# Order of the first loads in an attention and two-layer feed-forward kernel: queries in two parts, w_in ahead of the second batch's keys and values

## The chip, the core and the metric

The program runs on one core of one Trainium2 chip. The metric is the device time of one execution in microseconds (us), taken as the median of three runs. The engines are TensorE (PE, with its weight loads as PEld), VectorE (DVE), ScalarE (ACT), GpSimd (POOL) and SyncE (SP). SP issues nearly all DMA transfers, ACT a few; an engine takes its instructions in order.

## What is computed

Everything is float32 at the outside, the weights arrive as float64. Three stages follow one another:

```
k_p, v_p = mean of k, v over pools of 8 rows            # 576 rows -> 72
scores   = q @ k_p^T / sqrt(64); attn = softmax(scores)
x        = (attn @ v_p) laid out as 4608 tokens x 512    # 8 batches, 8 heads
h        = x @ w_in (512 x 2048);  g = h * cos(h);  y = g @ w_out
out      = (silu(y @ w_gate) * (y @ w_val)) @ w_out2
```

## The kernel before

Tokens are worked in nine blocks of 512, a batch has 576 of them. The first feed-forward layer runs as a list of slots (block, 128 columns of the hidden layer); the attention of the later batches is threaded between slots. The second layer follows. This document is about what comes ahead of slot 0 and about the first slots.

**Batches.** The code counts them from 0. The change's "batch 2" is index 1, written (1, ...) below. For batch 0 the queries come in by `load_q` (line 143): four transfers, for r and e in 0 and 1, each of 32 partitions and of rows of 32 floats (128 bytes). `ACT_QUEUE` (line 69) says which (batch, r) ACT issues, the rest go to SP. The keys and values of batch 0 go to `kst` and `vst`; those of batch 1 are loaded whole by `load_kv1` (line 171): four key tiles into the slots `wa30` to `wa33`, three value tiles into `wa20` to `wa22`, slots that later hold converted parts of w_in. Keys and values are pooled by adds on DVE (`pool_sum`, line 187). For batches 2 and up POOL does that.

**Tiles of attention.** Batch 0 has five tiles of queries. `do_qt` (254) transposes one on DVE, `do_s` (259) makes the scores on PE, their extreme on DVE and the exponentials on ACT, then come norms on DVE, transposes on PE with copies on ACT (`do_pt`), and the products with the values (`do_av`, 340) for a group of tiles, copied by ACT to `ring`. Scores, transposes and value products share two PSUM buffers. `x_split` (486) splits 512 tokens of `ring` into a high part (ACT) and a low part (DVE), and only then can `pe_h` (501), the first product of the feed-forward layer, run.

**Conversion of weights.** w_in and w_out are turned from float64 bits into float32 by hand: a unit is 128 rows by 512 columns, loaded by `cv_load` (432), then `cv_exp` and others on DVE, `cv_bias` and a copy on ACT. `conv` (952) is a generator over all units: eight of w_in ((0,0) to (0,3) and (1,0) to (1,3)), then w_out and w_in in turn. `fill(n)` (995) takes n steps of it, `fill_to` (999) goes on until a unit of w_in is done, `load_i(n)` (921) issues n units of w_in (two transfers of 256 KB each), `load_o(n)` (929) units of w_out. Slot 0 needs units (0,0) to (0,3); slots 4 to 7 need (1,0) to (1,3). Units (2,c) and (3,c) take the slots of the second batch's raw values and keys, so their load waits until those have been summed.

**Order.** The Python text gives a priority; a scheduler at build time sets each engine's order by priority and by when it believes operands to be ready, and puts in the waits, among them a wait of each transfer's issue for the landing of an earlier one that used the same semaphore. On the chip that order is fixed. The text ahead of slot 0 is lines 1008 to 1026, and then the string `program` (line 1057), whose words are calls: `s`, `x`, `p`, `a` for scores, norms, transposes and value products of batch 0; `V0 v` for its value sums; `f` and `F` for `fill` and `fill_to`; `i` and `o` for `load_i` and `load_o`; `X` for `x_split`; `q` for `load_q(1)`; `K` and `U` for the key and value sums of batch 1; `k` for its key transposes; `b` for the first load of batch 2.

Of the kernel before, what the change touches and what calls it, by code (L numbers as in the profile page):

```python
# [8 lines left out]
F32 = mybir.dt.float32  # L9
# [16 lines left out]
def fused_kernel(  # L26
# [18 lines left out]
    nc = tc.nc  # L45
    B, H, S, D = q.shape
# [3 lines left out]
    P = 128  # L50
    POOL = 8
    SP = S // POOL
    NP = H // 2
# [12 lines left out]
    LEAD = 4  # L66
    ACTB = 2
    Y32 = NF1
    ACT_QUEUE = {(0, 0), (3, 1), (1, 1), (3, 0), (1, 0)}

    const = ctx.enter_context(tc.tile_pool(name="const", bufs=1))
    chain = ctx.enter_context(tc.tile_pool(name="chain", bufs=2))
# [4 lines left out]
    p1a = tc.alloc_tile_pool(name="p1a", bufs=1, reuse_waits="tile")  # L77
# [62 lines left out]
    qt_in = {}  # L140
    qview = q.rearrange("b (r p) (t i) d -> b r i p t d", r=2, i=32)

    def load_q(b):
        qi = qt_in[b] = p1a.tile([P, NP, S], F32, name=f"qi_{b}", tag="qi")
        for r in range(2):
            for e in range(2):
                a = 32 * (2 * r + e)
                (nc.scalar if (b, r) in ACT_QUEUE else nc.sync).dma_start(
                    qi[a : a + 32].rearrange("i p (t d) -> i (p t) d", d=32),
                    qview[b, r, :, :, :, 32 * e : 32 * e + 32].rearrange("i p t d -> i (p t) d"),  # L150
                )

    kvraw = {}
    kraw1 = []
# [16 lines left out]
    def load_kv1():  # L171

        for p in range(NP):
            t = wts.tile([P, 2, TB], F32, name=f"k1_{p}", tag=f"wa3{p}")
            nc.sync.dma_start(t[:SP], kview[1][:, :, p].rearrange("r s x -> s r x"))
            kraw1.append(t[:SP])
        for j in range(0, NP + 1, 2):
            t = wts.tile([P, 2, TB], F32, name=f"v1_{j}", tag=f"wa2{j // 2}")
            for r in range(2):
                rows = t[r * SM : (r + 1) * SM]  # L180
                if j < NP:
                    nc.sync.dma_start(rows, vview[1][r, :, j : j + 2])
                else:
                    nc.sync.dma_start(rows[:, 0], vleft[1])
            vraw1.append((j, t[:, : min(2, NP + 1 - j)]))

    def pool_sum(eng, dst, raw):
        h = POOL * D // 2
        while h > D:
            eng.tensor_add(raw[..., :h], raw[..., :h], raw[..., h : 2 * h])  # L190
            h //= 2
        eng.tensor_add(dst, raw[..., :D], raw[..., D : 2 * D])
# [16 lines left out]
    def prep_k(b):  # L209

        kp = kps.pop(b)
        ps = psum.tile([P, NP, SP], F32, name=f"kps_{b}", tag="att", bufs=2)
        for p in range(NP):
            nc.tensor.transpose(ps[:, p], kp[:, p].rearrange("s r d -> s (r d)"), ident[:SP, :SP])
        nc.scalar.mul(kT[0:64, :, 0:SP], ps[0:64], -EXP_SCALE)
        nc.scalar.mul(kT[64:128, :, SP:], ps[64:128], -EXP_SCALE)
# [175 lines left out]
    def run_item(b, x):  # L392
        if x[0] == "s":
            do_s(b, x[1])
            if x[1] + 1 < len(TILES):
                do_qt(b, x[1] + 1)
        elif x[0] == "exp":
            do_exp(b, x[1])
        elif x[0] == "norm":
            do_norm(b, x[1])  # L400
        elif x[0] == "pt":
            do_pt(b, x[1])
        elif x[0] == "av":
            do_av(b, x[1], x[2])
            do_av(b, x[1], x[2] + 1)
        elif b + 1 < B:
            if x[0] == "q":
                load_q(b + 1)
            elif x[0] == "k":
                prep_k(b + 1)  # L410
            elif x[0] == "v":
                prep_v(b + 1)
            else:
                do_qt(b + 1, 0)
# [17 lines left out]
    def cv_load(key, src, home=None):  # L432
        st = raw_tile(f"st_{key}") if home is None else wts.tile([P, 2, TB], F32, name=f"st_{key}", tag=home)
        st = st.rearrange("p a t -> p (a t)")
        src = src if isinstance(src, list) else [src]
        m = P // len(src)
        for i, x in enumerate(src):
            nc.sync.dma_start(st[i * m : (i + 1) * m].bitcast(U64), x)
        cv[key] = st.rearrange("p (t two) -> p t two", two=2)
# [481 lines left out]
    def load_i(m):  # L921
        for _ in range(m):
            u = next(to_load_i, None)
            if u is not None:
                _, j, c = order[u]
                src = [w_in[(r * NP + c) * D : (r * NP + c + 1) * D, j * TB : (j + 1) * TB] for r in range(2)]
                cv_load(keys[u], src, f"wa{j}{c}")
# [67 lines left out]
    def fill(m):  # L995
        for _ in range(m):
            conv_done[0] = next(conv_ops, len(order))
# [12 lines left out]
        nc.sync.dma_start(kst4[:, r], kview[0][r])  # L1010
    load_i(1)
    fill(2)
    load_q(0)
    load_i(1)
    for r in range(2):
        nc.sync.dma_start(vst[r * SM : (r + 1) * SM, :NP], vview[0][r])
        nc.sync.dma_start(vst[r * SM : (r + 1) * SM, NP], vleft[0])
# [3 lines left out]
    for r in range(2):  # L1021
        pool_sum(nc.vector, kps[0][:, :, r], kst4[:, r])
    prep_k(0)
    load_kv1()
    load_i(1)
    fill(8)
    do_qt(0, 0)
    kfree = kst.rearrange("s h x -> s (h x)")
# [22 lines left out]
    def sum_v1():  # L1051
# [3 lines left out]


    program = (
        "s0 s1 f4 x0 s2 p0 V0 v x1 p1 f3 s3 a0 x2 p2 f3 x3 i1 p3 a1 w F3 X s4 i1 q o2 "
        "K0 K1 K2 K3 U0 x4 k b i3 f6 "
    )  # L1060
    steps = {
        "s": s_,
# [9 lines left out]
        "i": load_i,  # L1072
        "o": load_o,
        "q": lambda: load_q(1),
        "k": lambda: prep_k(1),
        "b": lambda: load_kv(*raws[0]),
# [22 lines left out]
    for i, s in enumerate(slots):  # L1099
        n, f = s  # L1100
# [157 lines left out]
```

## Time and profile before

| what | value |
|---|---|
| median of 3 runs | 1804.75 us (1804.24 to 1807.91) |
| profiled execution, its own time | 1804.83 us |
| its span in the profile | 1803.1 us |
| PE busy | 1737.5 us, 96% |
| DVE busy | 1263.8 us, 70% |
| ACT busy | 1066.6 us, 59% |

The span is what the profiler saw of the program; the time is the run's own and is 1.7 us longer. An engine's busy share is over the whole span; which engine holds up the others in a stretch has to be read from that stretch.

### The profile page before, as it was taken

To read this page: it belongs to the slowest core of one execution; us is meant where nothing else is said; L and a number is where in the kernel's file an instruction comes from. 1 tells how busy PE (TensorE), PEld (TensorE's weight loads), DVE (VectorE), ACT (ScalarE), POOL (GpSimd) and SP (SyncE) were. 2 spreads that over 40 slices of the span, in tenths; PEclk is the share of its full clock that TensorE was granted. 3 is DMA by queue.
4 is the path that set the end of the run, shared out by engine and by line. 5 is a ranking of instruction groups with operands and counts; after the bars stand their busy time and mean duration, and the time that the engine had idled before them with its cause. 6 is when DMAs were issued, how large, how long until landed. Compare 5 with 4: busy or idle time off the path is not lost.

```text
span 1803.1 us, 23421 instructions
## 1 busy us (share of the span) xinstructions
PE 1737.5 (96%) x8044; PEld 1439.4 (80%) x8044; DVE 1263.8 (70%) x2152; ACT 1066.6 (59%) x1933; POOL 171.7 (10%) x254
## 2 busy tenths in 40 slices
PE   2879999999999999999999999999999999999998
PEld 2546587888878888878877888888888888999998
DVE  6898688877877677787875586863584367358446
ACT  3578587777777767778776565533443344344333
POOL 0150513304104022000000000000000000000000
PEclk9989999999999999999999999999999999999999
DMA  9934246446566455474885488576667556787773
GB/s 186 203 104 120 79 165 188 156 131 197 148 205 218 114 198 144 158 220 153 235 275 176 159 320 291 193 252 225 194 200 267 193 192 221 290 265 246 294 249 93
DMA packets 248157, 357.01 MB, mean 198 GB/s; under 512 B 149608, under 2 KB 155752, under 8 KB 248040
## 3 DMA queue, kind: packets, MB, share of 16 engines
q1 hardware_dynamic: 224840, 352.58, 61.7%
q10 hardware_dynamic: 23200, 2.95, 1.1%
q8 instruction: 64, 1.05, 0.2%
q14 instruction: 53, 0.43, 0.1%
HBM read 285.74 MB, written 69.73 MB: 197 GB/s over the span
## 4 chain that ended last, share of the span: by engine, by line
PE 68%; DVE 14%; DMA 9%; ACT 5%; issue 2%; SPq 1%; POOL 0%; ACTq 0%; DVEq 0%
PE X L762 13%; PE oX L892 8%; PE Y L762 7%; PE h L507 4%; PE h L509 4%; PE h L508 4%; PE acc L578 4%; PE oY L892 4%; PE acc L579 4%; PE acc L577 4%; PE Z L762 3%; DMA w2r<-w_dram 2%; PE oZ L892 2%; PE av L358 2%; PE acc L570 2%
## 5 line engine op out<-in xcount | busy, mean ns | idle before, releaser
L762 PE MATMUL X<-t_P,wc 128*128 128x512 f32 (+1 forms) x1080 | 232.6, 367 | 1.0 <-ACT u L811 1.0
L507 PE MATMUL h<-xhl,wa 128*128 128x512 f32 x576 | 231.5, 402 | 0.0
L508 PE MATMUL h<-xhl,wa 128*128 128x512 f32 x576 | 226.3, 393 | 1.3 <-DVE xhl L131 1.3
L509 PE MATMUL h<-xhl,wa 128*128 128x512 f32 x576 | 225.6, 392 | 0.0
L762 PEld LDWEIGHTS X<-t_P,wc 128*128 128x128 f32 x1080 | 196.5, 188 | 27.5 <-ACT u L811 2.4
L578 PE MATMUL acc<-gl,wo_ring 128*128 128x512 f32 x448 | 176.4, 394 | 1.7 <-DVE gl L558 1.5
L577 PE MATMUL acc<-gh,wo_ring 128*128 128x512 f32 x448 | 175.1, 401 | 3.1 <-ACT gh L555 2.9
L579 PE MATMUL acc<-gh,wo_ring 128*128 128x512 f32 x448 | 175.4, 391 | 0.0
L544 DVE SCALAR_TENSOR_TENSOR w<-w,hs 128x512 f32<-128x512 f32 x144 | 102.3, 710 | 49.7 <-ACT w L541 48.4
L516 ACT ACTIVATE hs<-h 128x512 f32<-128x512 f32 x144 | 85.7, 595 | 76.4 <-DVE w L544 47.8
L540 ACT ACTIVATE w<-w 128x512 f32<-128x512 f32 x144 | 91.0, 632 | 64.9 <-DVE w L519 63.8
L507 PEld LDWEIGHTS h<-xhl,wa 128*128 128x128 f32 x576 | 108.7, 189 | 25.7 <-issue 4.1
L508 PEld LDWEIGHTS h<-xhl,wa 128*128 128x128 f32 x576 | 108.7, 189 | 25.3 <-issue 2.4
L509 PEld LDWEIGHTS h<-xhl,wa 128*128 128x128 f32 x576 | 108.5, 188 | 23.8 <-issue 0.9
L519 DVE SCALAR_TENSOR_TENSOR w<-w,hs 128x512 f32<-128x512 f32 x144 | 105.3, 731 | 23.7 <-ACT w L518 23.5
L814 DVE TENSOR_TENSOR p<-p,X 128x512 f32<-128x512 f32 (+1 forms) x60 | 37.9, 632 | 117.0 <-PE X L762 109.5
L558 DVE TENSOR_TENSOR gl<-w,gh 128x512 fp32r<-128x512 f32 x128 | 90.9, 710 | 40.2 <-ACT gh L555 38.6
L130 ACT CAST xhl<-pst 128x1024 fp32r<-128x1024 f32 (+1 forms) x70 | 67.7, 967 | 71.3 <-PE oX L892 26.1
L518 ACT ACTIVATE w<-hs,few 128x512 f32<-128x512 f32 x144 | 104.5, 725 | 7.3 <-DMA w_dram<-ce_w 4.2
L892 PE MATMUL oX<-xhl,wc 128*128 128x512 f32 (+1 forms) x480 | 102.8, 368 | 0.0
L578 PEld LDWEIGHTS acc<-gl,wo_ring 128*128 128x128 f32 x448 | 84.6, 189 | 21.5 <-DVE gl L558 5.2
L577 PEld LDWEIGHTS acc<-gh,wo_ring 128*128 128x128 f32 x448 | 84.1, 189 | 21.7 <-ACT gh L555 4.9
(197 smaller groups left out, 3586.3 us busy)
## 6 DMA issues: line engine op xcount, KB each, us to landing
wc<-wc_dram SPq DMA_DIRECT2D x273, 512.0 KB
wo_ring<-wo_dram SPq DMA_DIRECT2D x112, 512.0 KB
wc_dram<-wc SPq DMA_DIRECT2D x42, 512.0 KB
wc_dram<-ow SPq DMA_DIRECT2D x42, 256.0 KB
y_dram<-yo SPq DMA_DIRECT2D x18, 512.0 KB
w_dram<-ce_w SPq DMA_DIRECT2D x36, 256.0 KB
st_i<-in_moe_w_in_dram SPq DMA_DIRECT2D x32, 256.0 KB
st_o<-in_moe_w_out_dram SPq DMA_DIRECT2D x16, 512.0 KB
```

The source lines that it names most:

```text
L507: nc.tensor.matmul(ps, whi, xhl[:, 0, c], start=c == 0, stop=False)
L508: nc.tensor.matmul(ps, whi, xhl[:, 1, c], start=False, stop=False)
L509: nc.tensor.matmul(ps, wlo, xhl[:, 0, c], start=False, stop=c == KC - 1)
L518: nc.scalar.activation(w, h, AF.Identity, bias=magic)
L519: nc.vector.scalar_tensor_tensor(out=w, in0=w, scalar=MAGIC, in1=h, op0=ALU.subtract, op1=ALU.subtract)
L540: nc.scalar.activation(w, w, AF.Sin, scale=PI)
L544: nc.vector.scalar_tensor_tensor(out=w, in0=w, scalar=1.0, in1=h, op0=ALU.subtract, op1=ALU.mult, reverse0=True)
L577: nc.tensor.matmul(acc[n][i], a[:, cols], xh, start=f == 0, stop=False)
L578: nc.tensor.matmul(acc[n][i], a[:, cols], xl, start=False, stop=False)
L579: nc.tensor.matmul(acc[n][i], b[:, cols], xh, start=False, stop=f == NF1 - 1)
L762: nc.tensor.matmul(ps[:, :hb], w, t[:, x, c, :hb], start=first and c == 0 and n == 0, stop=c == 1 and n == 2, skip_group_check=not first,)
L892: nc.tensor.matmul(banks[key][m][:, :hb], u, x[:, b, i, :hb], start=first_ and j == i == k == 0, stop=j == NJ - 1 and i == 1 and k == 2, s ...
```

## The change

It has five parts. `load_q` can load a part of the tokens: for batch 0 the first 256 tokens are loaded alone, and the other 320 after one more unit of w_in; each part takes sixteen transfers of one head pair each (32 KB and 40 KB), half of them from ACT, half from SP. Both halves of batch 1's queries leave ACT's queue for SP's. `load_kv1` moves behind four units of w_in (1,0) to (1,3). The sums of batch 1's values (`U0`) move from behind the key sums to behind `f6 b i2`, with four more steps of conversion (`f4`) and one more unit's load after them. The calls of `i` are placed anew.

```
-    ACT_QUEUE = {(0, 0), (3, 1), (1, 1), (3, 0), (1, 0)}
+    ACT_QUEUE = {(0, 0), (3, 1), (3, 0)}
...
-    def load_q(b):
-        qi = qt_in[b] = p1a.tile([P, NP, S], F32, name=f"qi_{b}", tag="qi")
+    def load_q(b, cut=0, part=None):
+        if not part:
+            qt_in[b] = p1a.tile([P, NP, S], F32, name=f"qi_{b}", tag="qi")
+        lo, hi = (0, S // 32) if part is None else ((0, cut), (cut, S // 32))[part]
         for r in range(2):
             for e in range(2):
                 a = 32 * (2 * r + e)
-                (nc.scalar if (b, r) in ACT_QUEUE else nc.sync).dma_start(
-                    qi[a : a + 32].rearrange("i p (t d) -> i (p t) d", d=32),
-                    qview[b, r, :, :, :, 32 * e : 32 * e + 32].rearrange("i p t d -> i (p t) d"),
-                )
+                to = qt_in[b][a : a + 32].rearrange("i p (t d) -> i p t d", d=32)[:, :, lo:hi]
+                src = qview[b, r, :, :, lo:hi, 32 * e : 32 * e + 32]
+                eng = nc.scalar if (b, r) in ACT_QUEUE else nc.sync
+                if part is None:
+                    eng.dma_start(to.rearrange("i p t d -> i (p t) d"), src.rearrange("i p t d -> i (p t) d"))
+                else:
+                    for p in range(NP):
+                        eng.dma_start(to[:, p], src[:, p])
...
-    load_q(0)
+    load_q(0, 8, 0)
     load_i(1)
+    load_q(0, 8, 1)
...
     prep_k(0)
+    load_i(4)
     load_kv1()
-    load_i(1)
     fill(8)
...
-        "s0 s1 f4 x0 s2 p0 V0 v x1 p1 f3 s3 a0 x2 p2 f3 x3 i1 p3 a1 w F3 X s4 i1 q o2 "
-        "K0 K1 K2 K3 U0 x4 k b i3 f6 "
+        "s0 s1 f4 x0 s2 p0 V0 v x1 p1 f3 s3 a0 x2 p2 f3 x3 p3 a1 w F3 X s4 q o2 i1 "
+        "K0 K1 K2 K3 x4 k f6 b i2 U0 f4 i1 "
```

## Rows read from the trace of the kernel before

**Rows 1.** The page, part 1: busy time and share of the span of each engine.
```profile
PE 1737.5 (96%) x8044; PEld 1439.4 (80%) x8044; DVE 1263.8 (70%) x2152; ACT 1066.6 (59%) x1933; POOL 171.7 (10%) x254
```

**Rows 2.** Windows: stretch, length, busy us of each engine, granted clock, DMA share, GB/s.
```profile
0.00:24.00 24.00, 0.71 (x4) 0.53 (x4) 11.19 (x19) 4.66 (x7) 4.46 (x19) 1.00 0.99 179
24.00:45.00 21.00, 12.31 (x42) 9.47 (x42) 16.32 (x37) 12.81 (x64) 0.00 (x0) 1.00 0.94 195
45.00:72.00 27.00, 22.84 (x47) 10.71 (x47) 21.22 (x49) 13.10 (x36) 1.51 (x2) 1.00 0.97 213
72.00:90.00 18.00, 16.51 (x74) 12.26 (x74) 17.13 (x33) 11.15 (x35) 5.37 (x6) 1.00 0.83 187
90.00:140.00 50.00, 40.17 (x130) 23.27 (x129) 49.96 (x81) 38.33 (x96) 26.47 (x36) 0.90 0.35 106
140.00:200.00 60.00, 59.80 (x218) 36.21 (x217) 44.65 (x86) 47.90 (x112) 5.76 (x9) 1.00 0.34 91
```

**Rows 3.** Waits of DVE, 0 to 90 us: who waited for what, total, times, longest.
```profile
DVE mx L273 <- PE s L269: 4.6, 8, 1.5
...
DVE ce_i L456 <- ACT ce_i L451: 3.2, 3, 2.0
DVE wo L445 <- DMA st_i<-in_moe_w_in_dram: 2.1, 2, 1.7
DVE wo L445 <- DMA st_o<-in_moe_w_out_dram: 1.8, 2, 1.3
```

**Rows 4.** The chain that ended last, 0 to 60 us: start, length, what.
```profile
5.91 11.02 SPq L148
...
47.95 9.49 DMA qi<-in_q_dram
...
57.83 0.73 ACT ce_i L451
```

**Rows 5.** Timeline at 58 us: start, length, engine, line; in brackets idle time and releaser.
```profile
57.83 0.72 ACT L451 ACTIVATE ce_i<-ce_i,few 128x512 int32<-128x512 int32 x1 [4.55 <-DMA qi<-in_q_dram]
...
58.58 0.69 DVE L456 SCALAR_TENSOR_TENSOR ce_i<-st_i,ce_i 128x512 uint32<-128x512 uint32 x1 [2.03 <-ACT ce_i L451]
...
58.86 0.42 PE L330 MATMUL px<-ident,kst 128*64 128x128 f32 x1 [3.17 <-ACT ring L364]
```

**Rows 6.** Waits of SP's queue, 0 to 72 us.
```profile
SPq L438 <- DMA qi<-in_q_dram: 10.0, 1, 10.0
```

**Rows 7.** Timeline, 19 to 25 us: keys of batch 0 ready, first transpose, first scores.
```profile
19.42 0.41 ACT L216 ACTIVATE kT<-kps 64x288 f32<-64x288 f32 x1
...
23.81 0.70 DVE L257 STREAM_TRANSPOSE qT<-qi 128x512 f32<-128x512 f32 x1
...
24.66 0.58 PE L269 MATMUL s<-kT,qT 128*128 128x144 f32 x1 [5.78 <-DVE qT L257]
```

**Rows 8.** Issues of line 148, 0 to 180 us: durations in ns, least, median, most.
```profile
L148 ACTq DMA_DIRECT2D qi<-in_q_dram x6: 318/327/378, 0.8 to 61.4; - x6
L148 SPq DMA_DIRECT2D qi<-in_q_dram x6: 323/902/11024, 5.5 to 165.3; - x6
```

**Rows 9.** Timeline of SP, two rows.
```profile
41.47 9.06 SPq L438 DMA_DIRECT2D st_i<-in_moe_w_in_dram  x8
60.52 0.84 SPq L438 DMA_DIRECT2D st_o<-in_moe_w_out_dram  x2
```

**Rows 10.** Timeline: first key sum of batch 1, first product of slot 0.
```profile
41.17 0.64 DVE L190 TENSOR_TENSOR k<-k 72x512 f32<-72x512 f32 x1
...
71.54 0.80 PE L507 MATMUL h<-xhl,wa 128*128 128x512 f32 x1
```

**Rows 11.** Groups on DVE, 41 to 57 us: count, busy us, mean ns, idle before.
```profile
L190 DVE TENSOR_TENSOR k<-k 72x512 f32<-72x512 f32 (+1 forms) x8 | 4.1, 544 | 0.0
L190 DVE TENSOR_TENSOR v<-v 128x256 f32<-128x256 f32 (+2 forms) x6 | 2.9, 485 | 0.0
...
L192 DVE TENSOR_TENSOR vp<-v 128x128 f32<-128x128 f32 (+1 forms) x3 | 0.8, 266 | 0.1
```

## The prediction, made before the changed kernel was run

> **What bounds the kernel now.** I read the page first: PE is busy for 96% of the span [rows 1], so a change that takes no work from PE can win only where PE is idle. Then the windows, by stage [rows 2]. From 140 to 200 us PE is busy for 59.80 of 60 us; before that it is not. From 90 to 140 us it is DVE that has no gap, 49.96 of 50 us, and PE has 40.17. So two limits follow one another: DVE until about 140 us, PE after. DVE's work up to 140 us is a fixed amount (weight conversion, sums, softmax), and nothing in the change removes any of it. What the change can win is therefore DVE's idle time ahead of 90 us, and at about 140 us the whole of that gain is handed to PE. That idle time is 24.00 - 11.19 = 12.8 us up to 24, 4.7 us from 24 to 45, 5.8 us from 45 to 72 and 0.9 us from 72 to 90 us [rows 2]. The first piece is mostly the arrival of the first bytes, which stays. The next two pieces, 10.5 us, are the purse.
>
> What ends these gaps is in DVE's waits [rows 3]: 4.6 us for scores of PE in eight pieces, 3.2 us for an ACT step of the conversion, and 2.1 + 1.8 = 3.9 us for loads of w_in and w_out. The DMA engines are busy for 0.94 to 0.99 of the time up to 72 us [rows 2]: the beginning is fed by a full pipe, so what comes first in it matters, and nothing gets there sooner without something else coming later.
>
> The chain of waits and the timeline show the largest single stall [rows 4, 5]. ACT issues batch 1's queries. The first of these transfers takes 9.49 us, from 47.95 us, and ACT's next query issue waits for its landing. ACT does nothing for 4.55 us, and behind it on ACT stand a conversion step, a copy to the ring and a copy of the transposes: DVE then waits 2.03 us and PE 3.17 us. The same transfers hold SP: one issue of line 438 waits 10.0 us for a query transfer [rows 6], and the first two loads of w_out leave only at 60.52 us [rows 9].
>
> **The change, part by part.** I sum against the profiled execution's own 1804.83 us; its span is 1803.1, the other 1.7 us lie around it and are not touched. The median of the runs, 1804.75, is 0.08 us away, so the same sum holds for it.
>
> *Batch 1's queries from ACT to SP.* Four issues leave ACT, at 0.33 us each by the median [rows 8], 1.3 us, and with them the wait of 4.55 us. ACT is not the limit; what counts is DVE's share of it, 2.03 us [rows 5]. Bounds: nothing, if another late ACT step takes its place, and 3.17 us, if PE's share counts in full. I take -2.0 us, DVE's row, since DVE limits what follows. The Trainium skill ("DMA: Bandwidth & Descriptors", section "Issuing engines are not separate DMA queues") says that starting transfers on several engines saves only the issuing time, which is usually small. By that this part would be worth at most the issue time of four transfers; the row shows that the issuing engine can lose several times that when an issue must wait for a landing.
>
> *The loads behind them.* SP's wait of 10.0 us goes, but the four transfers now stand in SP's own queue ahead of w_out, and issues there have cost from 0.32 to 11.02 us, the last when one query transfer stood behind another [rows 4, 8]. So w_out and the units behind it come only somewhat earlier. DVE's 3.9 us of waits for them [rows 3] is the upper bound, nothing is the lower; I take half, -2.0 us.
>
> *Queries of batch 0 in two parts.* The first scores start at 24.66 us, after the transpose at 23.81 us; the keys were ready at 19.42 + 0.41 = 19.83 us [rows 7]. If the first 256 tokens are there by then, a transpose of 0.70 us puts the scores at about 20.5 us, 4.2 us sooner. PE's idle time then shrinks by that much, but DVE fills part of the same time with conversion already, and the later scores still alternate with ACT through two PSUM buffers. Bounds 0 and -4.2; I take -1.5 us, about a third of DVE's 4.6 us of waits for scores.
>
> *More and smaller transfers.* Four become 32, that is 28 more issues, 14 on each queue; at 0.32 to 0.33 us [rows 8] they take 4.6 us of each queue. SP sat for 11.02 us in one query issue at 5.91 us [rows 4], which hides its share if shorter transfers shorten that; ACT has done 4.66 us of work by 24 us [rows 2], which hides the other. If neither cover holds, 4.6 us lie on the path. I take +1.0 us, nearer to hidden, as both covers show in rows. The same page of the Trainium skill ("DMA: Bandwidth & Descriptors", section "Rules for kernel authors") speaks against this part: transfers under 64 KB are mostly overhead and should be joined. No row shows a query transfer that small; by the rule the sum would lose this part's gain and pay its upper bound, and that case is a rival below.
>
> *w_in ahead of batch 1's keys and values.* Eight issues of w_in took 9.06 us [rows 9]; four units now stand ahead of the keys, so these land about 9 us later and the four units earlier. The first key sum began at 41.17 us with no wait [rows 10, 11]. It is late by up to 9 us if DVE's order is unchanged; but DVE has conversion of the units that came first to do meanwhile, at up to 0.69 us an instruction [rows 5]. Bounds: +9 us (DVE stands at the key sum) and -1.9 us (the other half of the waits for loads). I take 0, because the key sums are needed only for batch 1's first scores, after slot 0's first product at 71.54 us [rows 10].
>
> *Batch 1's value sums later.* 2.9 + 0.8 = 3.7 us of DVE work [rows 11] move behind `f6`; they are not removed, and DVE has no gap later on, so 0. Behind them, though, wait the loads of units (2,c), whose slots hold these values: bounds 0 and +1.7 us, the longest wait of DVE for such a load now [rows 3]. I take 0, as the value sums have no other wait than their own landing.
>
> *The four extra steps of conversion and the moved `i` calls* change priorities alone: 0, covered by the same DVE work being done in another order.
>
> Sum: -2.0 - 2.0 - 1.5 + 1.0 = -4.5 us, so 1804.83 - 4.5 = 1800.3 us.
>
> **The rivals.**
>
> *The pipe is the limit (same).* With the DMA engines at 0.94 to 0.99 up to 72 us [rows 2], a reordering moves waits from one load to another: DVE waits for batch 1's keys instead of for w_out. For it: that share. Against it: the ACT hold is no lack of bytes, and a unit of w_in gives DVE more work per byte than the values do (six instructions of up to 0.69 us for 512 KB, against 3.7 us for 1,280 KB). It keeps -2.0 and pays back most: about 1804 us.
>
> *Late keys (slower).* The scheduler leaves the key sums where they are in DVE's order, and DVE, in order, stands at line 190 until they land, with the split of the first 512 tokens and the conversion queued behind. The price is what DVE waits there, up to 9.06 us [rows 9]: 1800.3 + 9.1 = 1809.4 us. It decides when that wait passes 4.5 us, and shows as slower by 0.2% past 8.1 us. For it: DVE's order is fixed at build time and the sums had no slack shown but 0.0 idle [rows 11]. Against it: the scheduler knows that the loads were moved.
>
> *Small query transfers hold ACT and SP (slower).* Each issue still waits for an earlier landing, and ACT's sixteen stand among the steps that write the keys at 19.42 us [rows 7]. Two holds of 4.55 us [rows 5], one for each part, less what the other terms give: 9.1 + 1.0 - 4.0 = +6.1, about 1811 us. Against it: ACT is nearly empty until 24 us [rows 2]. This is also where the skill's rule on small transfers would lead: 4.6 us on the path and no gain gives 1804.83 - 4.0 + 4.6 = 1805.4 us.
>
> *The order does not come out as written.* The scheduler may put the value sums or the loads where they were; then the ACT and SP parts alone stay: about 1801 us.
>
> **How the numbers follow.** About 0.2%, 3.6 us, is what a measurement of this kernel can tell from no change. Chances: the forecast 0.57 (most of it past 3.6 us, about an eighth of it short of that), the pipe 0.20, late keys 0.09, small transfers 0.10, order not as written 0.04. Faster by more than 0.2%: 0.52. Slower: most of late keys and of small transfers, 0.18. Within 0.2%: 0.30. The low end takes the bounds of the three gains nearly together, -3.2 - 3.9 - 4.2 = -11.3, less than all of it: 1794. The high end stops inside the slower rivals: 1807. Likeliest case alone: 1796 to 1803 us.
>
> **What would show each step.** In the changed trace: the first scores at 20 to 22 us; no ACT wait for a query landing near 58 us; the loads of w_out issued before 60 us; no DVE wait at line 190 for keys; DVE busy in 24 to 72 us for some 4 us more of an equal stretch, or the first product near 66 us in place of 71.54 us [rows 10]; a gapless PE from about 135 us. The prediction is wrong if DVE's waits for landings up to 90 us are as long as before, if the query issues hold ACT ahead of the keys, or if DVE's stretch without gaps ends no sooner.

## The result and the profile after

The changed kernel takes 1825.24 us (median of four runs, 1823.79 to 1828.35), the kernel before 1804.49 us beside it (four runs). The ratio is 1.0115, 95% interval 1.0102 to 1.0127: 20.7 us **slower**. The prediction of 1800.3 us, with 1794 to 1807, is wrong in size and in sign. The profiled execution took 1826.17 us; its span is 1824.2 us.

The page first, for what has not changed. An engine's work is nearly that of [rows 1]: DVE 4.8 us more, PE 5.2 us more, with the same counts of instructions. So the engines do the same work; what grew is mostly the gaps between it. (PE's 5.2 us come back in the last section.)

```profile
PE 1742.7 (96%) x8044; PEld 1440.3 (79%) x8044; DVE 1268.6 (70%) x2152; ACT 1071.0 (59%) x1933; POOL 169.8 (9%) x254
```

The windows of the changed kernel say where the gaps are. The columns are those of [rows 2]: stretch and its length, busy time (with counts) of PE, PEld, DVE, ACT and POOL, granted clock of TensorE, DMA share, GB/s.

```profile
0.00:24.00 24.00, 0.71 (x4) 0.53 (x4) 11.79 (x19) 4.66 (x7) 4.48 (x19) 1.00 0.77 154
24.00:45.00 21.00, 12.20 (x42) 9.50 (x42) 12.21 (x30) 11.26 (x61) 0.00 (x0) 1.00 0.95 213
45.00:72.00 27.00, 21.75 (x45) 10.44 (x46) 16.85 (x31) 12.53 (x36) 0.00 (x0) 1.00 0.79 165
72.00:90.00 18.00, 14.89 (x68) 10.60 (x66) 15.02 (x37) 10.43 (x33) 0.00 (x0) 0.95 0.19 49
90.00:140.00 50.00, 34.36 (x113) 22.64 (x114) 39.26 (x78) 35.75 (x85) 4.46 (x6) 0.81 0.37 97
140.00:200.00 60.00, 53.63 (x172) 28.96 (x171) 53.94 (x91) 42.10 (x98) 26.41 (x34) 0.97 0.54 156
```

Read the third busy column. From 24 to 140 us, 116 us, DVE was busy for 16.32 + 21.22 + 17.13 + 49.96 = 104.6 us before [rows 2], so it was idle for 11.4 us. Now it is busy for 12.21 + 16.85 + 15.02 + 39.26 = 83.3 us and idle for 32.7 us. That is 21.3 us more idle time, and the kernel is 20.7 us slower. The stretch from 90 to 140 us, in which DVE had no gap, now has 10.7 us of them, and DVE's work spills past 140 us (53.94 us busy there, 44.65 us before). PE, busy for 59.80 of the 60 us from 140 us on before, now has 53.63. The DMA share from 72 to 90 us is 0.19 where it was 0.83: bytes are not what is missing there.

What DVE waits for, 0 to 140 us of the changed kernel (who for what: total, times, longest), answers to [rows 3]. The change makes the code longer, so the lines named here stand 7 lower than before: the load of w_in and w_out, 438 before, is now 445, and the first step of their conversion on DVE, 445 before, is now 452.

```profile
DVE mx L280 <- PE s L276: 13.2, 10, 3.4
DVE ce_i L463 <- ACT ce_i L458: 9.0, 5, 4.8
DVE ce_i L452 <- DMA st_i<-in_moe_w_in_dram: 6.5, 2, 6.3
DVE w L551 <- ACT w L548: 5.1, 4, 1.6
...
DVE w L526 <- ACT w L525: 2.9, 2, 1.5
```

One of these is a transfer, and 6.3 of its 6.5 us are the very first load of w_in, before 7 us, which the kernel before waits for too. From 24 to 140 us no wait of DVE is for a transfer. The 3.9 us of waits for w_out and w_in at line 445 [rows 3] are gone, as wanted, and DVE stands at no key of batch 1. It waits for other engines instead, at steps that now follow one another with nothing between. Waits of SP's queue over the same stretch show the reverse side: SP, which waited for a query transfer [rows 6], now waits for DVE, which has not yet freed the buffers that the next loads go into.

```profile
SPq L445 <- DVE vp L199: 23.6, 2, 21.2
SPq L445 <- DVE mx L280: 20.2, 1, 20.2
SPq L445 <- DVE wo L480: 16.4, 1, 16.4
```

The timeline of the changed kernel, single lines of ACT, PE, SP and DVE in order of time (start, length, engine, line; in brackets idle time and releaser):

```profile
10.84 1.38 SPq L445 DMA_DIRECT2D st_i<-in_moe_w_in_dram  x2
...
18.08 0.72 ACT L458 ACTIVATE ce_i<-ce_i,few 128x512 int32<-128x512 int32 x1 [9.25 <-DMA qi<-in_q_dram]
...
24.35 2.02 PE L276 MATMUL s<-kT,qT 128*128 128x144 f32 x7 [6.19 <-DVE qT L264]
...
38.77 3.32 SPq L182 DMA_DIRECT2D k<-in_k_dram  x4
...
61.66 1.92 SPq L445 DMA_DIRECT2D st_o<-in_moe_w_out_dram  x2
...
75.08 1.95 DVE L197 TENSOR_TENSOR k<-k 72x512 f32<-72x512 f32 x4
...
84.89 1.15 SPq L445 DMA_DIRECT2D st_i<-in_moe_w_in_dram  x2
...
97.33 0.69 DVE L526 SCALAR_TENSOR_TENSOR w<-w,hs 128x512 f32<-128x512 f32 x1 [1.42 <-ACT w L525]
99.38 0.69 DVE L551 SCALAR_TENSOR_TENSOR w<-w,hs 128x512 f32<-128x512 f32 x1 [1.36 <-ACT w L548]
101.56 0.69 DVE L526 SCALAR_TENSOR_TENSOR w<-w,hs 128x512 f32<-128x512 f32 x1 [1.48 <-ACT w L525]
103.61 0.69 DVE L551 SCALAR_TENSOR_TENSOR w<-w,hs 128x512 f32<-128x512 f32 x1 [1.36 <-ACT w L548]
...
104.40 0.60 ACT L523 ACTIVATE hs<-h 128x512 f32<-128x512 f32 x1 [0.82 <-DVE w L551]
...
104.85 0.39 DVE L452 TENSOR_SCALAR wo<-st_o 128x512 uint32<-128x512 uint32 x1
...
132.28 0.60 ACT L523 ACTIVATE hs<-h 128x512 f32<-128x512 f32 x1
```

And the same place in the kernel before, DVE's timeline from 101 us:

```profile
101.03 0.94 DVE L456 SCALAR_TENSOR_TENSOR wo<-st_o,wo 128x512 uint32<-128x512 uint32 x1
...
102.15 0.97 DVE L462 TENSOR_SCALAR st_o<-st_o 128x512 uint32<-128x512 uint32 x1
103.04 0.68 DVE L445 TENSOR_SCALAR wo<-st_o 128x512 uint32<-128x512 uint32 x1
103.64 0.80 DVE L467 SCALAR_TENSOR_TENSOR st_o<-st_o 128x512 f32<-128x512 uint32 x1
104.36 0.68 DVE L987 TENSOR_TENSOR wa<-wo,wa 128x512 fp32r<-128x512 f32 x1
104.96 1.21 DVE L519 SCALAR_TENSOR_TENSOR w<-w,hs 128x512 f32<-128x512 f32 x1
```

These two lists show what goes wrong. Before, between two DVE steps of a slot (line 519 and its like), DVE converts weights, and the time that ACT needs for the slot's cosine is covered. After, slots 2, 3 and 4 follow one another at 4.2 us (their first ACT steps come at 95.94, 100.17 and 104.40 us) with nothing in between, and DVE stands 1.4 us before each step. The conversion of w_out that could have filled these gaps begins only at 104.85 us, though its load was issued at 61.66 us. Then the neglected conversion is made up, and slot 5 starts 27.9 us after slot 4 (8.1 us before). The key sums tell the same: issued at 38.77 us, summed at 75.08 us, against 41.17 us before [rows 10]. DVE never stood waiting for those keys, so it is not the data that were late; DVE's fixed order put other instructions first.

DVE's order differs in over 200 of its first 450 places. Six steps, their places counted in DVE's instructions from the program's start:

| DVE step | place before | place after |
|---|---|---|
| first key sum of batch 1 | 49 | 82 |
| value sums of batch 1 | 72 to 83 | 102 to 117 |
| split of the first 512 tokens | 104 | 74 |
| first conversion step of w_out's first unit | 96 | 128 |
| first conversion step of unit (2,0) | 102 | 138 |
| first step of slot 0 / slot 3 / slot 4 | 125 / 169 / 189 | 107 / 125 / 165 |

### The profile page after: what moved, and what is told of

Same layout as the page of the kernel before. It is cut to its first block, busy times and chain, and to the rows that moved or that the text cites. A ratio compares the mean times of both kernels' runs of the same rounds, so it can differ in the third digit from the quotient of the medians.

```text
span 1824.2 us, 23457 instructions
## 1 busy us (share of the span) xinstructions
PE 1742.7 (96%) x8044; PEld 1440.3 (79%) x8044; DVE 1268.6 (70%) x2152; ACT 1071.0 (59%) x1933; POOL 169.8 (9%) x254
## 4 chain that ended last, share of the span: by engine, by line
PE 71%; DVE 14%; ACT 6%; DMA 6%; issue 2%; SPq 0%; ACTq 0%; DVEq 0%
PE X L769 14%; PE oX L899 8%; PE Y L769 7%; PE h L514 4%; PE h L515 4%; PE h L516 4%; PE acc L585 4%; PE acc L584 4%; PE acc L586 4%; PE oY L899 4%; PE Z L769 3%; PE av L365 3%; PE oZ L899 2%; DMA w2r<-w_dram 2%; PE s L276 2%
## 5 line engine op out<-in xcount | busy, mean ns | idle before, releaser
L525 ACT ACTIVATE w<-hs,few 128x512 f32<-128x512 f32 x144 | 104.6, 726 | 9.9 <-DMA w_dram<-ce_w 6.0
L197 POOL TENSOR_TENSOR kraw<-kraw 72x256 f32<-72x256 f32 x96 | 79.2, 825 | 281.7 <-DMA kraw<-in_k_dram 277.9
L585 PEld LDWEIGHTS acc<-gl,wo_ring 128*128 128x128 f32 x448 | 84.2, 188 | 22.2 <-DVE gl L565 5.9
```

The costliest lines, as they stand in the source:

```text
L525: nc.scalar.activation(w, h, AF.Identity, bias=magic)
L585: nc.tensor.matmul(acc[n][i], a[:, cols], xl, start=False, stop=False)
```

## The experiments

### One part of the change taken back

Four kernels, each the changed one with one part as before. If one part carries the loss, taking it back returns most of 20.7 us.

**Keys and values ahead of the four units again.**

```diff
-    load_i(4)
     load_kv1()
+    load_i(4)
```

> The changed kernel with the second batch's keys and values again ahead of the four units of w_in; all else as changed. Theory L (late sums: because those loads stand later, the build puts that batch's key and value sums behind the first products in DVE's order, so DVE has holes before 72 us and the loads into the values' slots wait on SP for 21 us): most of the 20.7 us comes back, 1803 to 1808 us, SP's long wait for the value sums under 5 us. Theory Q (the small query transfers and their landings hold ACT and DVE): no change, 1822 to 1826 us. Theory U (the value sums' place in the text): no change, 1822 to 1826 us.

Measured: 1831.7 us, ratio 1.0141 (1.0126 to 1.0156). Worse than the changed kernel, by some 5 us, which no theory had. Late keys are not the cause.

**The value sums at their old place.**

```diff
-        "K0 K1 K2 K3 x4 k f6 b i2 U0 f4 i1 "
+        "K0 K1 K2 K3 U0 x4 k f6 b i2 f4 i1 "
```

> The changed kernel with the value sums (U0) again right behind the key sums in the text. Theory U: the sums come before the first products, the wait on SP falls from 21.2 us to under 5 us, 1804 to 1810 us. Theory L: the order that the build gives DVE stays what it was, since readiness and not the text sets it, so 1823 to 1828 us and the same 21 us wait. Theory Q: 1823 to 1828 us.

Measured: 1827.02 us, 1.0121 (1.0099 to 1.0142), the same as the changed kernel. With `U0` at either place the build gives every engine the very same instructions and waits in the same order: it is the same program, so this part of the change does nothing, and 20.7 and 21.8 us are two measurements of one thing. SP's wait of 21.2 us for the value sums is real, but the place of `U0` did not bring it.

**Batch 0's queries whole.**

```diff
-    load_q(0, 8, 0)
+    load_q(0)
     load_i(1)
-    load_q(0, 8, 1)
```

> The changed kernel with batch 0's queries in four whole transfers again. Theory Q: 10 to 20 us come back, 1805 to 1815 us, with the ACT wait of 9.2 us for a query landing gone and DVE's waits for scores back from 13 to about 5 us. Theory L: the long wait on SP stays at about 20 us, 1820 to 1828 us. Theory U: 1823 to 1828 us.

Measured: 1827.19 us, 1.0116 (1.0100 to 1.0132). Nothing came back, so theory Q fails: the split is not what makes the changed kernel slow.

**Batch 1's queries on ACT again.**

```diff
-    ACT_QUEUE = {(0, 0), (3, 1), (3, 0)}
+    ACT_QUEUE = {(0, 0), (3, 1), (1, 1), (3, 0), (1, 0)}
```

> The changed kernel with batch 1's queries again on ACT's queue. If taking them from ACT is worth the 2.0 us that I forecast, this is that much slower, 1826 to 1829 us. If SP's queue behind those four transfers costs more than ACT's hold did, it is faster, 1818 to 1823 us. Theory L: value sums stand some 16 places earlier in DVE's order in this build, so the wait on SP shrinks by several us and the time falls with it, 1815 to 1823 us. Theories Q and U: no more than 2 us either way.

Measured: 1821.17 us, 1.0088 (1.0071 to 1.0105). About 5 us come back (its four executions spread from 1813.88 to 1823.21 us), the most of the four, and three quarters of the loss stay. No single part, taken back, undoes it.

### One part done alone

**Batch 1's queries on SP, all else as before** (the same line as above, the other way).

> The kernel before with one edit: batch 1's queries on SP's queue instead of ACT's. Theory S (with four slow query transfers ahead of w_out on SP, the build ranks the first conversions of w_out and of the later w_in behind slots 0 to 3 in DVE's fixed order, so those slots run early and then DVE, SP and PE stand): most of the loss is there by this edit alone, 1818 to 1828 us; slots 0 to 3 some 4 us apart, then a gap of over 20 us before slot 5. Theory L in its second form (w_in ahead of the keys and values): 1801 to 1805 us. My forecast's own step: -2 to -4 us, 1800 to 1803 us.

Measured: 1825.02 us, 1.0111 (1.0094 to 1.0127). One line, which changes who issues four transfers, loses as much as the whole change, as theory S had it: slots 1 to 4 start 4.2 us apart, and slot 5 comes 28 us later.

**Four units of w_in ahead of the keys alone**, with the two `i1` of the program's first line dropped:

```diff
+    load_i(4)
     load_kv1()
-    load_i(1)
...
-        "s0 s1 f4 x0 s2 p0 V0 v x1 p1 f3 s3 a0 x2 p2 f3 x3 i1 p3 a1 w F3 X s4 i1 q o2 "
+        "s0 s1 f4 x0 s2 p0 V0 v x1 p1 f3 s3 a0 x2 p2 f3 x3 p3 a1 w F3 X s4 q o2 "
```

> The kernel before with one edit: four units of w_in ahead of batch 1's keys and values, the two later loads of w_in dropped. Theory S: close to before, 1801 to 1810 us, since w_out's conversion keeps its place in DVE's order. Theory L in its second form: 1815 us or more, because the units behind the values' slots are converted in DVE's order ahead of slot 0 but land late, and DVE waits for them.

Measured: 1814.51 us, 1.0052 (1.0035 to 1.0069), between the two ranges. Here DVE does stand for transfers: 10.0 us for loads of w_out and 5.0 us for w_in at line 445, 1.8 and 2.1 us before [rows 3].

**Batch 0's queries in two parts alone** (`load_q` and its calls as in the change):

> The kernel before with one edit: batch 0's queries in two parts of sixteen transfers each. Theory S: 1803 to 1810 us, a few us lost as the pipe is emptier in the first 24 us (the changed kernel moved 154 GB/s there, before 179) and ACT stands 9 us in a query issue. Theory Q: over 1812 us. My forecast's own step: -0.5 us.

Measured: 1821.01 us, 1.0084 (1.0066 to 1.0103). Over 1812 us, as theory Q had it, and outside what S and the forecast allowed. Each of these three parts loses alone, 9 to 20 us, and together they lose no more than the first. (The extra conversion steps and the moved calls were not run alone.) Prices of separate waits would add up; these do not. That points to something that all of them set off, which the runs further down put to the test.

**Batch 1's queries on SP, but behind w_out in the text**, to see whether it is SP's queue ahead of w_out that hurts:

```diff
-    ACT_QUEUE = {(0, 0), (3, 1), (1, 1), (3, 0), (1, 0)}
+    ACT_QUEUE = {(0, 0), (3, 1), (3, 0)}
...
-        ... F3 X s4 i1 q o2 "
-        "K0 K1 K2 K3 U0 x4 k b i3 f6 "
+        ... F3 X s4 i1 o2 "
+        "K0 K1 K2 K3 U0 x4 k b i3 q f6 "
```

> The kernel before with batch 1's queries on SP as in the run before, but called behind the first loads of w_out and three more units of w_in. Theory S: w_out's first conversion is 15 places earlier in DVE's order and ACT's hold of 4.6 us is gone, so the loss of the run before goes and 1800 to 1806 us stand. If instead the four transfers cost their time on SP wherever they stand: within 5 us of the run before it.

Measured: 1827.12 us, 1.0117 (1.0097 to 1.0137). w_out's loads now leave at 49.19 us, 11 us sooner than before [rows 9], and the time is as bad. An earlier w_out doesn't help, then, and where the queries stand on SP's queue makes no difference. That is also what the second expectation said (within 5 us), by a price of the transfers themselves; the run with three orders held, below, shows that price to be near nothing.

What the change and these eight share is DVE's idle time from 24 to 140 us, worked out as above. It is read from one profiled execution of each, the time from several; for the queries on ACT back the profiled execution was the fastest of the four, 1813.88 us. The change and the kernel with the value sums back are one program, and so are two kernels of the second table; their idle times differ by 0.9 and 2.6 us, and closer than that the two columns can't be compared.

| kernel | idle, us more than before | time, us more (ratio - 1, of 1805) |
|---|---|---|
| the change | 21.3 | 20.7 |
| keys back | 26.5 | 25.5 |
| value sums back | 22.2 | 21.8 |
| queries whole | 19.6 | 20.9 |
| queries on ACT back | 13.3 | 15.9 |
| queries on SP alone | 21.6 | 20.0 |
| w_in ahead alone | 12.2 | 9.4 |
| queries in two alone | 17.0 | 15.2 |
| queries on SP, behind w_out | 17.5 | 21.1 |

### Loads and orders crossed

The scheduler gives each of these kernels, but the one with the value sums back, another order of DVE than the change has, and all of them another than before. To part the order from the loads, the text of a kernel stays and its first 450 DVE instructions are held to another kernel's order by edges that add no wait, only a sequence. What is not held, SP's queue among it, the scheduler orders anew:

```
for a, b in zip(places, places[1:]):     # places: the other kernel's order
    tc.add_manual_dep(seq[b], seq[a].name,
        mybir.DependencyInfo(mybir.DependencyClass.NoSync, mybir.DependencyReason.DATA), reason="order")
```

**The changed loads, DVE in the order of before:**

> The changed kernel, all its loads as changed, but its first 450 DVE instructions held by issue-order edges to the order that they have in the kernel before. Theory O (the loss is the order that the build gives DVE, in which some 20 us of holes open before 140 us; the new loads themselves cost little): most of the 20.7 us comes back, 1802 to 1812 us, DVE idle from 24 to 140 us near 15 us in place of 32.6. Theory T (the new places and sizes of the loads are the loss): DVE now stands for landings at its old places, 1818 us or more.

Measured: 1815.79 us, 1.0056 (1.0036 to 1.0077), between the two ranges. Half of the loss is gone, and DVE's wait of 8.0 us for a key load is what theory T had.

**The loads of before, DVE in the order of after:**

> The reverse: the kernel before, its loads unchanged, but its first 450 DVE instructions held to the order of the changed kernel. Theory O: the loss is there without any changed load, 1818 to 1830 us, with slots 0 to 3 about 4 us apart and then a gap. Theory T: 1803 to 1810 us.

Measured: 1824.68 us, 1.0108 (1.0093 to 1.0123). Not one load, queue or transfer differs in the text from the kernel before, and the time is that of the change. Its windows from 24 to 140 us:

```profile
24.00:45.00 21.00, 12.04 (x42) 9.22 (x41) 13.08 (x30) 12.25 (x67) 0.00 (x0) 1.00 0.92 183
45.00:72.00 27.00, 19.17 (x39) 9.19 (x40) 15.96 (x30) 10.21 (x26) 2.28 (x3) 1.00 0.91 192
72.00:90.00 18.00, 17.80 (x73) 12.87 (x72) 14.82 (x36) 8.70 (x33) 4.32 (x3) 1.00 0.42 102
90.00:140.00 50.00, 30.07 (x93) 18.92 (x93) 37.76 (x63) 31.14 (x73) 24.68 (x37) 0.76 0.38 108
```

DVE's column reads like the changed kernel's (12.21, 16.85, 15.02, 39.26), not like that of before: 34.4 us idle. Slots 1 to 4 start 4.2 us apart and slot 5 comes 34 us later. **The order makes the loss, with no load edited.** Only DVE's order was held; ACT, PE and SP got from the scheduler what goes with it. SP's transfers leave in the order of before up to 59 us, and after that part of them in another.

**Batch 1's queries on SP, DVE in the order of before:**

> The kernel before with batch 1's queries on SP's queue, its first 450 DVE instructions held to the order before. Theory O: the loss of 20 us that this edit made alone goes, and my forecast's step is seen by itself: ACT's hold of 4.55 us and DVE's 2.03 us behind it gone, 1799 to 1805 us. Theory T: 1815 us or more, as w_out lands behind four query transfers.

Measured: 1808.58 us, 1.0021 (1.0012 to 1.0031), between the two ranges.

**Queries in two parts, DVE in the order of before:**

> The kernel before with batch 0's queries in two parts of sixteen transfers each, its first 450 DVE instructions held to the order before. Theory O: most of the 16 us that this edit lost alone comes back, 1803 to 1809 us. Theory T: 1815 us or more; the pipe is emptier in the first 24 us and that delays all behind it.

Measured: 1808.3 us, 1.0021 (1.0011 to 1.0031), as theory O had it. Three quarters and more of what the two parts lost alone (20.0 and 15.2 us) go with the order. The rest has a face in DVE's waits of the first of the two, where 3.2 us stood before [rows 3]:

```profile
DVE ce_i L456 <- ACT ce_i L451: 13.9, 3, 12.7
```

One ACT conversion step came 12.7 us late, since ACT still ran in its own new order (10.6 us in the kernel with the changed loads). With one engine held, the other two can keep orders that don't match it, as in these two kernels. (With the queries in two parts they came out as before by themselves.) So the next five hold ACT (420 instructions) and PE (700) as well.

**The changed loads, all three engines in the order of before:**

> The changed kernel with the first 450 DVE, 420 ACT and 700 PE instructions held to their order in the kernel before; the loads are as changed. Theory O in full (the loss is the order of DVE and ACT): 1802 to 1808 us, DVE's wait of 10.6 us for an ACT step gone. Theory T (late landings at the old places): it stays at 1812 us or more, and DVE stands 8 us for a key load as in the run with DVE's order alone held.

Measured: 1809.51 us, 1.0019 (1.0008 to 1.0030): +3.4 us in place of +20.7, between the two ranges, with the wait for an ACT step gone as theory O had it and the wait for a key load there as theory T had it. Its windows, and the one wait of DVE that is new:

```profile
24.00:45.00 21.00, 12.31 (x42) 9.46 (x42) 13.58 (x31) 11.82 (x57) 0.00 (x0) 1.00 0.94 202
45.00:72.00 27.00, 16.83 (x35) 7.88 (x36) 21.19 (x52) 8.31 (x30) 0.00 (x0) 1.00 0.99 201
72.00:90.00 18.00, 18.00 (x63) 11.76 (x64) 15.67 (x32) 14.40 (x40) 3.04 (x3) 1.00 0.74 170
90.00:140.00 50.00, 40.45 (x139) 24.02 (x137) 48.23 (x75) 36.61 (x97) 29.61 (x40) 0.90 0.39 117
```

```profile
DVE k L197 <- DMA k<-in_k_dram: 9.0, 1, 9.0
```

With the old order the late-keys rival appears as forecast, a wait of 9.0 us against a bound of 9.06 [rows 9], at line 197, which was 190. DVE's idle time is 17.3 us, 5.9 us more than before, so about a third of that wait was made up in other gaps.

**Batch 1's queries on SP, three orders held:**

> The kernel before with batch 1's queries on SP's queue, DVE, ACT and PE held to their old order. Theory O and my forecast's step: ACT's hold of 4.55 us gone, nothing else moved, 1800 to 1804 us. Theory T: 1807 us or more, as w_out and the later units of w_in land behind the queries and DVE stands for them.

Measured: 1804.03 us, 0.9996 (0.9986 to 1.0006), no difference: -0.7 us, from -2.5 to +1.1. So the one line that lost 20.0 us loses nothing once the orders are held, and holding them costs nothing that shows here. ACT's stand of 4.55 us [rows 5] is gone, but DVE now waits longer for w_out, 1.8 us before [rows 3]:

```profile
DVE wo L445 <- DMA st_o<-in_moe_w_out_dram: 4.0, 2, 2.3
```

**Queries in two parts, three orders held:**

> The kernel before with batch 0's queries in two parts of sixteen transfers each, DVE, ACT and PE held to their old order. Theory O: 1803 to 1806 us. Theory T: 1807 to 1812 us, since the pipe moved 155 GB/s in the first 24 us in place of 179, and what is loaded after is late by 3 us or so.

Measured: 1807.61 us, 1.0014 (1.0000 to 1.0027): +2.5 us, in theory T's range. Since ACT and PE had come out in their old orders already with DVE's held, this is the same program as there, measured again: +3.8 us the first time, +2.5 us now. Together they show a small loss.

**w_in ahead of the keys, three orders held:**

> The kernel before with four units of w_in ahead of batch 1's keys and values, DVE, ACT and PE held to their old order. Theory T: DVE's key sums keep their old place, 41 us, and their loads land 9 us later, so 1809 to 1815 us with a wait of DVE for a key load of about 8 us. Theory O: 1803 to 1808 us.

Measured: 1809.36 us, 1.0023 (1.0010 to 1.0037): +4.2 us, in theory T's range. DVE waits 4.6 us for a key tile at line 190, about half of what that theory had, and for w_out only 0.3 us, where it waited 10.0 us with this edit in the order that the build gave it.

**An attempt at a better kernel: batch 1's queries from GpSimd's queue, three orders held.** If the held order keeps the loss away and SP's queue gives the gain back, an idle queue should bring it.

```diff
-                (nc.scalar if (b, r) in ACT_QUEUE else nc.sync).dma_start(
+                (nc.gpsimd if b == 1 else nc.scalar if (b, r) in ACT_QUEUE else nc.sync).dma_start(
```

> The kernel before with all four transfers of batch 1's queries issued from GpSimd's queue, which has nothing else to do there, and the orders of VectorE, ScalarE and TensorE held to before's. Theory O (the order is the loss, what a load's queue costs by itself is small): neither ScalarE's stand of 4.5 us nor SyncE's of 10.0 us at a query issue is left, so up to 5 us of VectorE's 11.4 us of idle time before 140 us go; 1799 to 1805 us, not slower than before. Rival (the pipe is the limit: a load that comes sooner makes another come later): VectorE's waits for w_out or the keys grow by what the holds free; within 2 us of before.

Measured: 1809.23 us, 1.0014 (1.0005 to 1.0023): +2.5 us, outside what the first theory allowed, and within its interval where the rival put it. DVE's waits, 0 to 140 us:

```profile
DVE ce_i L445 <- DMA st_i<-in_moe_w_in_dram: 9.0, 2, 6.9
...
DVE wo L445 <- DMA st_o<-in_moe_w_out_dram: 6.0, 3, 2.9
```

The wait for w_out is 6.0 us where it was 1.8 [rows 3], and w_in's has a second piece, of some 2 us. With neither ACT nor SP held by the queries, DVE still waits for loads, and longer. That speaks for the pipe as the limit of the loads by themselves (its DMA share is 1.02 from 45 to 72 us). No version was found that clearly beats the kernel before.

The same account for the nine kernels with held orders:

| kernel | engines held | idle, us more | time, us more |
|---|---|---|---|
| changed loads, old order | DVE | 11.1 | 10.1 |
| old loads, changed order | DVE | 23.0 | 19.5 |
| queries on SP | DVE | 6.3 | 3.8 |
| queries in two | DVE | 6.7 | 3.8 |
| changed loads | DVE, ACT, PE | 5.9 | 3.4 |
| queries on SP | DVE, ACT, PE | 0.4 | -0.7 |
| queries in two | DVE, ACT, PE | 4.1 | 2.5 |
| w_in ahead | DVE, ACT, PE | 5.3 | 4.2 |
| queries on GpSimd | DVE, ACT, PE | 5.4 | 2.5 |

## Why the prediction was wrong

**What held.** The unit of account: idle time that DVE gains ahead of 140 us passes nearly one for one into the time. Over the change and the first eight kernels the two columns agree within 3.6 us; over the nine with held orders within 3.5 us, the time always a little the smaller. That is shown for idle time added; no run took any away, so whether the prediction's 10.5 us could be won is not shown. In the changed kernel DVE is busy for 29.1 us from 24 to 72 us, 8.5 us less than before, where the prediction had looked for some 4 us more.

**The step that failed** is the last and shortest of the sum: the four extra steps and the moved calls "change priorities alone: 0, covered by the same DVE work being done in another order". The same work in another order cost 19.5 us with the loads of before, and the old order took 17.3 of the changed kernel's 20.7 us away again (20.7 - 3.4). The order alone (19.5) and the loads alone (3.4) add up to 22.9 us, the loss within the intervals. And it was not those calls alone, which no run tried by themselves: every other term was worked out as if DVE's order stood still while a load moved. In this kernel it doesn't. Moving who issues a load, or how large its transfers are, sets another order of three engines at build time. The order rival had the right place, "does not come out as written", with the wrong price (about 1801 us, since it let the gains of the ACT and SP parts stand). That the scheduler orders by priority and by when it believes operands to be ready stood in the description of the kernel; the prediction drew on it once, as comfort, that the scheduler "knows that the loads were moved", and priced nothing by it.

The other terms, now with orders held:

- *Queries from ACT to SP*, -2.0, and *the loads behind them*, -2.0: together -0.7 us (-2.5 to +1.1). ACT's hold vanished as forecast; the wait for w_out grew by 2.2 us and took its place. In the changed kernel w_out's loads left at 61.66 us, where the prediction had looked for them before 60 us. With the measured interval -4.0 is excluded. The Trainium skill's statement in "DMA: Bandwidth & Descriptors", section "Issuing engines are not separate DMA queues", that issuing from more engines saves only the issuing time, agrees with this -0.7 us; the prediction set it aside for one row.
- *Queries in two parts*, -1.5, and *smaller transfers*, +1.0: +2.5 us (0 to +4.9) and +3.8 us (+2.0 to +5.6), two measurements of one program. The first scores came at 24.35 us, forecast 20 to 22, before 24.66 [rows 7]. ACT stood 9.25 us at a query issue until an earlier query transfer had landed, so the small-transfers rival's hold was there; SP issued its second unit of w_in only at 10.84 us; and the first 24 us moved 154 GB/s in place of 179 [rows 2]. The Trainium skill's rule in "DMA: Bandwidth & Descriptors", section "Rules for kernel authors", that transfers under 64 KB are mostly overhead, points the same way as these numbers.
- *w_in ahead of the keys*, 0: +4.2 us (+1.8 to +6.7), nearer the middle of its bounds, -1.9 and +9. In the changed kernel itself this wait does not exist, for the order had moved the key sums past it.
- *Value sums later*, 0: the right number for another reason than the one given, since the edit changes nothing in the program.

**The rivals.** Late keys shows clearly only where the order is held (9.0, 8.0 and 4.6 us). The pipe is what the waits of the run from GpSimd's queue and the -0.7 us speak for, and its 1804 us would have been a fair forecast for the query loads in a kernel that keeps its order. Of the slower rivals none came near 1825 us.

**What stays open.** Why the scheduler ranks the sums and w_out's conversion so late is argued and not shown. In the changed kernel and in the four with the queries on SP ahead of w_out (keys back, value sums back, queries whole, queries on SP alone), w_out's first conversion stands at place 128; it stands at 96 before, at 103 with the queries back on ACT, at 113 with them behind w_out. That fits a scheduler that believes w_out to land behind the queries, but its belief was not read. Nor is a late w_out what all the losing orders have in common: with w_in ahead alone and with the queries in two alone its first conversion stands at 100 and 98, close to before, and they lose 9.4 and 15.2 us. What each moved step costs in those orders was not parted. And +3.4 us of the changed loads were measured as a whole; its three parts, at -0.7, +2.5 and +4.2, fit it only within their intervals.

## What to carry to other kernels

Where a scheduler sets the engines' order, an edit to a load is an edit to the order of every engine: price the order first, by comparing the built orders, and only then the loads. Hold the old order and change the loads, and hold the old loads and change the order; those two runs said more here than eight that undid or did one part. And a loss that each of several small edits brings alone, and that does not add up, is a sign of something they all set off.

## What the runs showed beside that

- From 90 to 140 us TensorE's granted clock is 0.81 in the changed kernel and 0.76 with its order alone, against 0.90 before [rows 2] and 0.90 for the changed loads with three orders held, while PE was busy for 34.36, 30.07, 40.17 and 40.45 us of those 50. They are means over a stretch, between the two levels. Fewer busy microseconds do not always go with a lower clock: with the queries on ACT back, PE is busy for 7.19 of the 18 us from 72 to 90 us, and the clock there is 1.00.
- The loss lies all in the beginning. The last 1603 us of the span hold 1585.16 us of PE's work before and 1584.50 us after. In what comes ahead of them, 200 us before and 221 us after, PE is busy for 152.34 and 158.20 us with nearly the same products (510 and 512). So some 15 of the 21 us are PE's gaps, and some 6 are products that took longer, at a mean granted clock of 0.95 in place of 0.97. What the lower clock cost by itself was not tried.
- Holding one engine's order of three left waits of 10.6 and 12.7 us for an ACT step in two kernels; with all three held the longest is 3.5 us.
- Earlier w_out loads (49.19 us, with the queries behind them) won nothing, and an idle issuing queue won nothing: of the beginning's 11.4 us of DVE idle time, no reordering of loads tried here took any that can be measured.
